# Second expert layer with one 512-column product per hidden slice, and new durations in the planner

## The chip, the cores and the metric

The kernel runs on one core of a Trainium2 chip. The metric is device time in microseconds (us) of one execution; shown is the median of several runs. Engines go by the names of the profile: PE is TensorE (PEld its weight loads), DVE is VectorE, ACT is ScalarE, POOL is GpSimd, SP issues most of the transfers.

## The reference, cut to what matters

Two stages. The first mixes tokens in the frequency domain: x of shape (8, 2496, 256) goes through a real FFT along the sequence, a complex 256 x 256 matrix with bias, a soft threshold and the inverse FFT. The second is a mixture of 8 experts with greedy routing of all 19968 tokens, and that is what the change touches:

```python
cap = N // E                              # 2496 tokens for each expert
order = np.argsort(-logits.flatten())     # best (token, expert) pair first
# a pair is taken if the token is free and the expert has room
for e in range(E):
    mask = assigned == e
    h = np.maximum(x[mask] @ w1[e], 0.0)  # 256 -> 1024
    out[mask] = h @ w2[e]                 # 1024 -> 256
```

## The kernel before, in words

**Stages.** `phase_a` does the spectral part batch by batch with products against DFT matrices, through DRAM scratch tensors T1 and T2, and writes the mixed tokens to YD and their gate logits to LG. `Router` finds, by counting and bisecting on VectorE (`count`, `search`, `bisect`), which tokens each expert gets. `Experts` gathers those tokens, runs both layers and scatters the rows to the output.

**Experts.** There are 16 jobs: for each expert an early one of 512 tokens, from the first half of the batches, and then a late one of 1984 tokens. A job is cut into chunks of up to 512 tokens. `fetch` gathers tiles of 128 tokens (L597, on POOL). `xpose` transposes them (L614), and ScalarE and VectorE split the result into a high and a low part (L617, L618). `ffn1` makes one slice of 128 hidden units with three products of up to 512 columns for each half of the 256 inputs (L629): high weights x high tokens, high x low, low x high. ScalarE writes the rectified high part hh (L633), VectorE the low part hl (L634). `ffn2` makes the output of one tile of 128 tokens: four steps (`qr`) of two hidden slices each, three products of 256 columns per slice, into one PSUM tile `pso` (L646); then ScalarE copies it to SBUF (L650) and POOL scatters it by an indirect transfer (L654). `pso` has two buffers, the output tile `os` has eight.

```python
for a, w_ in ((hh, 0), (hh, 1), (hl, 0)):
    T.matmul(ps.t[0:M], lhsT=a.t[:, 128 * q:128 * q + M], rhs=W2.t[:, w_, ft], start=k == 0, stop=k == 23)
```

W2 holds the high half of the weights as `W2[:, 0]` and the low half as `W2[:, 1]`, eight slices of 256 columns each.

**Order of the work.** The order on every engine is fixed when the program is built. `Plan.run` simulates the engines: each task has an engine, an assumed duration, a position `pos`, and what it reads and writes. At each step it gives the engine that is free first the task that can start first, ties going by `pos`, and for VectorE and POOL within a small hold. The instructions are emitted in that order, and each engine works its queue off in it. So an assumed duration moves no instruction's own time, but can move the order. `K.t` adds a task for TensorE, `v` one for VectorE with 0.068 + n/960 us, `plan.add('A', ...)` one for ScalarE.

**Start.** Batch 0's input comes in 6 chunks of 3 transfers (L1038). Where `(c + j) % 2` is odd they are issued by ScalarE's queue, else by SP's, in the order of the chunks; the DFT matrix for them is issued by ScalarE first (L938). The first DFT (L1062) goes through two PSUM buffers `p15`, which ScalarE and VectorE empty in turn (L1072, L1074). SP stores the results to T1 (L1077) and loads them back transposed as `sh` (L1083); the second DFT (L1096) reads `sh`. L1115 is the product with the complex weights.

**Lists.** For a late job `lists` turns a prefix sum into token numbers: products L479 and L496, sign activations and copies on ScalarE (L501, L502), and some arithmetic on VectorE that ends in the list `li` (L510, L511).

## Time and profile before

| | us |
|---|---|
| median of 3 runs | 1575.0 (1574.66 to 1575.14) |
| the profiled execution | 1583.92 |
| its span, first to last instruction | 1582.1 |
| PE busy in it | 1534.2 |
| DVE busy | 1076.8 |
| ACT busy | 856.0 |
| POOL busy | 669.2 |

The profiled execution is longer than the runs shown by 8.9 us. Products are pipelined, so that the duration of one (about 280 ns for 256 columns) is longer than the distance from its start to that of the next, and a busy PE is not one at its peak. The distance between starts is what a product costs in a stream. Idle time of an engine that is not the bound costs nothing by itself.

### The profile page before, as it was taken

To read this page: it belongs to the slowest core of one execution; us is meant where nothing else is said; L and a number is where in the kernel's file an instruction comes from. 1 tells how busy PE (TensorE), PEld (TensorE's weight loads), DVE (VectorE), ACT (ScalarE), POOL (GpSimd) and SP (SyncE) were. 2 spreads that over 40 slices of the span, in tenths; PEclk is the share of its full clock that TensorE was granted. 3 is DMA by queue.
4 is the path that set the end of the run, shared out by engine and by line. 5 is a ranking of instruction groups with operands and counts; after the bars stand their busy time and mean duration, and the time that the engine had idled before them with its cause. 6 is when DMAs were issued, how large, how long until landed. Compare 5 with 4: busy or idle time off the path is not lost.

```text
span 1582.1 us, 31579 instructions
## 1 busy us (share of the span) xinstructions
PE 1534.2 (97%) x10967; PEld 1362.7 (86%) x10967; DVE 1076.8 (68%) x3451; ACT 856.0 (54%) x1870; POOL 669.2 (42%) x891
## 2 busy tenths in 40 slices
PE   7999999999899989999899999999999999999998
PEld 4999999999787866888788989988998989979997
DVE  3677667677985654789988889887877765453321
ACT  2768888787678776444535234344343443553332
POOL 2236566564636644221334334434334344333332
PEclk8999999999999999999999999999999999999999
DMA  8777777877668666333213122121311212311110
GB/s 256 194 242 248 220 248 215 255 234 229 222 200 257 191 204 182 124 107 114 91 38 101 44 66 71 49 87 55 97 37 51 87 52 83 106 46 42 44 48 28
DMA packets 144201, 208.24 MB, mean 132 GB/s; under 512 B 28751, under 2 KB 108575, under 8 KB 144030
## 3 DMA queue, kind: packets, MB, share of 16 engines
q1 hardware_dynamic: 126776, 161.02, 33.1%
q0 software_dynamic: 16656, 43.77, 8.9%
q8 instruction: 88, 1.44, 0.4%
q10 hardware_dynamic: 598, 1.33, 0.3%
q14 instruction: 83, 0.68, 0.2%
HBM read 121.31 MB, written 84.75 MB: 130 GB/s over the span
## 4 chain that ended last, share of the span: by engine, by line
PE 79%; DVE 7%; DMA 5%; issue 5%; ACT 2%; POOL 1%; SPq 0%; ACTq 0%; POOLq 0%; DVEq 0%
PE ps L646 25%; PE ps L629 16%; PE ps L1115 10%; PE p L629 8%; PE ps L1096 4%; PE ps L1131 3%; PE p L1055 2%; PE p L1162 2%; PE ps L614 2%; PE pt L1185 2%; PE p L1166 1%; PE p L496 1%; PE ps L1203 1%; DVE junk L414 1%; POOL out_dram L654 1%
## 5 line engine op out<-in xcount | busy, mean ns | idle before, releaser
L1115 PE MATMUL ps<-wt,xTh 128*128 128x256 f32 x1280 | 243.4, 288 | 0.2 <-DVE y L1123 0.2
L1115 PEld LDWEIGHTS ps<-wt,xTh 128*128 128x128 f32 x1280 | 198.8, 189 | 8.1 <-issue 3.0
L1115 PE MATMUL ps<-wt,xTl 128*128 128x256 f32 x640 | 179.0, 280 | 0.0
L654 POOL DMA_INDIRECT out_dram<-xTh,li x64 | 65.7, 1026 | 264.6 <-ACT xTh L650 236.4
L414 DVE SCALAR_TENSOR_TENSOR junk<-h_m,st,h_AG 128x156 bf16<-128x156 f32 (+1 forms) x472 | 159.0, 384 | 2.8
L932 POOL TENSOR_TENSOR zl<-y,zh 128x512 fp32r<-128x512 f32 x80 | 106.7, 1334 | 117.3 <-ACT zh L929 110.3
L1192 POOL TENSOR_TENSOR yTl<-yr,yTh 128x468 bf16<-128x468 f32 (+1 forms) x88 | 97.5, 1109 | 93.6 <-ACT yTh L1191 85.1
L1115 PEld LDWEIGHTS ps<-wt,xTl 128*128 128x128 f32 x640 | 120.5, 188 | 0.2 <-DVE xTl L1108 0.2
L654 POOL DMA_INDIRECT out_dram<-xTl,li x64 | 66.0, 1032 | 92.9 <-ACT xTl L650 75.7
L1096 PE MATMUL ps<-FG,sh 128*128 128x128 f32 x640 | 98.0, 282 | 4.5 <-DMA sh<-T 4.5
L646 PE MATMUL ps<-FG,yTh 128*128 128x256 f32 x464 | 97.9, 282 | 0.0
L1096 PEld LDWEIGHTS ps<-FG,sh 128*128 128x128 f32 x640 | 87.4, 194 | 11.9 <-DMA sh<-T 4.7
L650 ACT COPY xTl<-ps 128x256 f32<-128x256 f32 x80 | 29.8, 372 | 124.7 <-PE ps L646 104.6
L646 PE MATMUL ps<-FG,y 128*128 128x256 f32 (+1 forms) x444 | 96.8, 281 | 0.0
L932 POOL TENSOR_TENSOR s2l<-s2c,s2h 120x512 fp32r<-120x512 f32 (+2 forms) x60 | 77.7, 1300 | 35.9 <-DVE s2h L929 27.0
L650 ACT COPY xTh<-ps 128x256 f32<-128x256 f32 x80 | 29.9, 374 | 110.9 <-PE ps L646 93.2
L932 DVE TENSOR_TENSOR xl<-xt,xh 117x512 fp32r<-117x512 f32 (+1 forms) x66 | 66.9, 1015 | 23.8 <-ACT xh L929 23.0
L1106 DVE TENSOR_TENSOR xTl<-ps,xTh 128x512 fp32r<-128x512 f32 x80 | 54.8, 685 | 39.0 <-ACT xTh L1105 38.3
L646 PEld LDWEIGHTS ps<-FG,yTh 128*128 128x128 f32 x464 | 73.3, 185 | 1.4 <-issue 0.2
L646 PE MATMUL ps<-FG,s2c 128*128 128x256 f32 (+1 forms) x336 | 74.1, 281 | 0.0
L646 PEld LDWEIGHTS ps<-FG,y 128*128 128x128 f32 (+1 forms) x444 | 72.2, 185 | 1.9
L646 PE MATMUL ps<-FG,yTl 128*128 128x256 f32 (+1 forms) x312 | 73.8, 280 | 0.0
(708 smaller groups left out, 5053.3 us busy)
## 6 DMA issues: line engine op xcount, KB each, us to landing
xt<-in_moe_w_dram SPq DMA_DIRECT2D x64, 512.0 KB
T<-s4st SPq DMA_DIRECT2D x80, 256.0 KB
sh<-T SPq DMA_DIRECT2D x39, 512.0 KB
s2c<-T SPq DMA_DIRECT2D x80, 240.0 KB
YD<-yst SPq DMA_DIRECT2D x80, 234.0 KB
T<-s1st SPq DMA_DIRECT2D x73, 240.0 KB
xt<-in_x_dram SPq DMA_DIRECT2D x105, 156.0 KB
LG<-lgst SPq DMA_DIRECT2D x80, 21.9 KB
```

The source lines that it names most:

```text
L414: v(cols + 59 + 1400 * K.extra, p, lambda k=k: V.scalar_tensor_tensor(junk[k % 2].t[:, 0:cols], H.m[:, 0:cols], c.t[:, k // ng:k // ng + 1 ...
L614: T.transpose(ps.t[:, 128 * q:128 * q + 128], xg[t // 2].t[:, t % 2, 128 * m:128 * m + 128], H.idn)
L629: T.matmul(ps.t[:, 0:w], lhsT=W1.t[:, a, m, 128 * ft:128 * ft + 128], rhs=x_.t[:, 0:w], start=q + m == 0, stop=q + m == 3)
L646: T.matmul(ps.t[0:M], lhsT=a.t[:, 128 * q:128 * q + M], rhs=W2.t[:, w_, ft], start=k == 0, stop=k == 23)
L650: plan.add('A', .27, pos + 1, lambda: A.copy(o.t[0:M], ps.t[0:M]), [ps], [o])
L654: ins = P.indirect_dma_start(out=self.out, out_offset=bass.IndirectOffsetOnAxis(ap=oi.t[0:M, oo + t:oo + t + 1], axis=0), in_=o.t[0:M], in ...
L932: lambda: eng.tensor_tensor(lb[1](), src(), hb[1](), op=OP.subtract), [srcb, hb[0]], [lb[0]])
L1096: T.matmul(ps.t[:, i, 128 * dt:128 * dt + 128], lhsT=sh.t[:, k, 128 * dt:128 * dt + 128], rhs=Ft.t[:, k], start=True, stop=True)
L1106: plan.add('V', dve(512), pos, lambda th=th, tl=tl, src=src, apart=apart: apart(V.tensor_tensor(cols(tl, 64, 192), src(), cols(th, 64, 192 ...
L1115: T.matmul(ps3.t[:, i], lhsT=a.t[:, i, dt, o:o + 128], rhs=wt[c].t[:, w, dt], start=n == 0, stop=n == 11)
L1131: T.matmul(ps4.t[:, i], lhsT=Gt[p // 8].t[:, g, (2 * p + i) % 16], rhs=v.t[:, i], start=n == 0, stop=n == 2)
L1192: yq.append(plan.add('P', pool(2 * W), pos + 0.376, lambda yh=yh, yl=yl, yr=yr, W=W: P.tensor_tensor(yl.t[:, :, 0:W], yr.t[:, :, 0:W], yh. ...
```

## The change

In `ffn2` a hidden slice now takes two products instead of three. The high part hh is loaded once and multiplied with both halves of the weights in one product of 512 columns, whose result fills a whole PSUM bank: columns 0 to 255 get hh x high weights, columns 256 to 511 hh x low weights. The low part hl times the high weights is accumulated onto the first half as before. ScalarE copies the second half to the output tile, then VectorE adds the first half to it in place. The token `ob` makes the addition wait for the copy.

Assumed durations of the planner are changed in many places, and batch 0's input loads are now all issued by SP.

```diff
         def ffn2(c, q, pos):
...
-            ps, o = K.psum("pso", [128, 256]), K.sb("os", [128, 256])
+            ps, o = K.psum("pso", [128, 2, 256]), K.sb("os", [128, 256])
+            ob = plan.buf(None, None)
             for qr in range(4):
                 def mm(qr=qr):
-                    k = 6 * qr
                     for ft in range(2 * qr, 2 * qr + 2):
-                        hh, hl = hT[c, ft]
-                        for a, w_ in ((hh, 0), (hh, 1), (hl, 0)):
-                            T.matmul(ps.t[0:M], lhsT=a.t[:, 128 * q:128 * q + M], rhs=W2.t[:, w_, ft], start=k == 0, stop=k == 23)
-                            k += 1
-                last = K.t(.652, pos + .5 * qr, mm, [W2] + [x for ft in range(2 * qr, 2 * qr + 2) for x in hT[c, ft]], [ps])
+                        hh, hl = [a.t[:, 128 * q:128 * q + M] for a in hT[c, ft]]
+                        if ft == 7: T.matmul(ps.t[0:M, 0], lhsT=hl, rhs=W2.t[:, 0, ft], start=False, stop=False)
+                        T.matmul(ps.t[0:M], lhsT=hh, rhs=W2.t[:, :, ft], start=ft == 0, stop=ft == 7)
+                        if ft < 7: T.matmul(ps.t[0:M, 0], lhsT=hl, rhs=W2.t[:, 0, ft], start=False, stop=False)
+                last = K.t(.696, pos + .5 * qr, mm, [W2] + [x for ft in range(2 * qr, 2 * qr + 2) for x in hT[c, ft]], [ps])
             self.steps.append(last)
-            plan.add('A', .27, pos + 1, lambda: A.copy(o.t[0:M], ps.t[0:M]), [ps], [o])
+            plan.add('A', .27, pos + 1, lambda: A.copy(o.t[0:M], ps.t[0:M, 1]), [ps], [o, ob])
+            v(256, pos + 1, lambda: V.tensor_tensor(o.t[0:M], ps.t[0:M, 0], o.t[0:M], op=OP.add), [ps, ob], [o])
...
-                turn = not b and (c + j) % 2
-
-                def em(t=t, j=j, m=m, g0=g0, turn=turn):
+                def em(t=t, j=j, m=m, g0=g0):
...
-                    (nc.scalar if turn else nc.sync).dma_start(t.t[39 * j:39 * j + 39, 0:m, :], src)
+                    nc.sync.dma_start(t.t[39 * j:39 * j + 39, 0:m, :], src)
```

The other assumed durations, before and after: the count products .12 to .146; in `lists` the first product .1 to .12, the list products .09 n to .083 + .058 n, the signs .29 to .385 (plus the columns), the copies .06 to .15; the spacer copy on POOL .15 to .28; a chunk's transposes .118 n to .083 + .089 n; an `ffn1` step 3w/2400 + .012 to .018 + 3w/2286; in the early lists .09 nt to .083 + .037 nt; the closing's two small products .05 to .146; in the spectral stage the split after a ScalarE copy + .2, the DFT products 3n/2400 + .02 to .028 + 3n/2286, the complex product 1.42 to 1.47, the rectifying activation + .1, the inverse product 0.715 to 0.745, the transposes 0.42 to 0.4, the gate products .47 + .12 each to .62 + .04 each.

## Rows read from the trace of the kernel before

**Rows 1.** The page: busy us of each engine, share of the span, instructions.
```profile
PE 1534.2 (97%) x10967; PEld 1362.7 (86%) x10967; DVE 1076.8 (68%) x3451; ACT 856.0 (54%) x1870; POOL 669.2 (42%) x891
```

**Rows 2.** Busy us in two stretches: stretch, length, PE, PEld, DVE, ACT, POOL, PEclk, DMA share, GB/s.
```profile
0.00:31.70 31.70, 21.43 (x60) 8.56 (x60) 8.49 (x48) 6.33 (x10) 5.75 (x16) 0.93 0.82 235
...
300.00:400.00 100.00, 98.39 (x799) 90.62 (x798) 73.76 (x124) 80.20 (x159) 57.17 (x46) 1.00 0.75 226
```

**Rows 3.** The page: the chain that ended last, by engine and by line.
```profile
PE 79%; DVE 7%; DMA 5%; issue 5%; ACT 2%; POOL 1%; SPq 0%; ACTq 0%; POOLq 0%; DVEq 0%
PE ps L646 25%; PE ps L629 16%; PE ps L1115 10%; PE p L629 8%; PE ps L1096 4%; PE ps L1131 3%; PE p L1055 2%; PE p L1162 2%; PE ps L614 2%; PE pt L1185 2%; PE p L1166 1%; PE p L496 1%; PE ps L1203 1%; DVE junk L414 1%; POOL out_dram L654 1%
```

**Rows 4.** Copies of finished tiles, L650: count, ns min/median/max, first and last start, forms.
```profile
L650 ACT COPY xTh<-ps x80: 362/373/385, 626.7 to 1572.4; 128x256 f32<-128x256 f32 x80
L650 ACT COPY xTl<-ps x80: 363/373/385, 627.4 to 1575.2; 128x256 f32<-128x256 f32 x72, 64x256 f32<-64x256 f32 x8
```

**Rows 5.** Pieces of the chain that ended last: start us, us, what, how many products.
```profile
635.12 2.73 PE ps L629 x12
...
640.82 2.75 PE ps L629 x12
...
647.11 1.39 PE p L629 x6
...
945.97 9.90 PE ps L646 x84
```

**Rows 6.** Groups of VectorE: shape, count, busy us, mean ns, idle before.
```profile
L1108 DVE TENSOR_TENSOR xTl<-xTh,ps 128x256 fp32r<-128x256 f32 x80 | 32.7, 409 | 0.0
```

**Rows 7.** Busy us from 660 to 960, all engines, columns as in the second group.
```profile
660.00:960.00 300.00, 293.77 (x1977) 259.88 (x1976) 265.93 (x1162) 128.56 (x275) 99.39 (x160) 0.99 0.26 85
```

**Rows 8.** The same stretch for L646 alone: PE, PEld, PEclk, DMA share, GB/s.
```profile
660.00:960.00 300.00, 148.39 (x1152) 142.69 (x1152) 0.99 0.26 85
```

**Rows 9.** All engines from 740 to 760, columns as in the second group.
```profile
740.00:760.00 20.00, 18.17 (x126) 15.48 (x126) 19.89 (x62) 9.31 (x21) 5.08 (x7) 1.00 0.28 84
```

**Rows 10.** Timeline of the end: start, us, engine, line, operation, idle before and releaser.
```profile
1575.16 0.37 ACT L650 COPY xTl<-ps 64x256 f32<-64x256 f32 x1 [2.43 <-PE ps L646]
1575.80 0.91 POOL L654 DMA_INDIRECT out_dram<-xTl,li  x1 [1.73 <-ACT xTl L650]
```

**Rows 11.** Timeline of the start; SPq and ACTq are issues of transfers.
```profile
0.75 0.84 SPq L1038 DMA_DIRECT2D xt<-in_x_dram  x2
...
1.43 0.31 ACTq L1038 DMA_DIRECT2D xt<-in_x_dram  x1
1.63 6.79 SPq L1038 DMA_DIRECT2D sh<-in_x_dram  x7
...
1.78 9.29 ACTq L1038 DMA_DIRECT2D sh<-in_x_dram  x8
...
11.10 1.28 ACT L1072 ACT_TABLE_LOAD   x1 [11.10 <-DMA sh<-in_x_dram]
...
13.03 9.16 PE L1062 MATMUL p<-sh,xh 117*120 117x512 f32 x16 [3.13 <-ACT s4st L1072]
...
26.22 3.09 SPq L1083 DMA_DIRECT2D sh<-T  x6
...
31.73 0.58 PE L1096 MATMUL ps<-FG,sh 128*128 128x128 f32 x1 [4.52 <-DMA sh<-T]
```

**Rows 12.** The page: transfer queues, packets, MB, share of 16 engines' span.
```profile
q1 hardware_dynamic: 126776, 161.02, 33.1%
...
q10 hardware_dynamic: 598, 1.33, 0.3%
```

**Rows 13.** Waits of PE: total us, times, longest.
```profile
PE p L496 <- ACT jl L502: 5.8, 6, 2.6
```

**Rows 14.** Timeline around one list: its last step, and the first transposes after it.
```profile
981.02 0.17 DVE L511 TENSOR_SCALAR li<-li 128x6 int32<-128x6 f32 x1
...
992.53 0.38 PE L614 MATMUL ps<-h_idn,y 128*128 128x128 f32 x2
```

More of the change, by code (lines that the diff above doesn't have):

```diff
@@ L614, in tr @@
                         T.transpose(ps.t[:, 128 * q:128 * q + 128], xg[t // 2].t[:, t % 2, 128 * m:128 * m + 128], H.idn)
-                K.t(.118 * nt, pos + .5 * m, tr, [H.b_idn] + [xg[t] for t in range(2 * c, 2 * c + (nt + 1) // 2)], [ps])
+                K.t(.083 + .089 * nt, pos + .5 * m, tr, [H.b_idn] + [xg[t] for t in range(2 * c, 2 * c + (nt + 1) // 2)], [ps])
                 w = 128 * nt
@@ L630, in ffn1 @@
             for m in range(2):
-                last = K.t(3 * w / 2400 + .012, pos + .5 * m, lambda m=m: mm(m), [W1] + xT[c][m], [ps])
+                last = K.t(.018 + 3 * w / 2286, pos + .5 * m, lambda m=m: mm(m), [W1] + xT[c][m], [ps])
             self.steps.append(last)
```

36 lines of the change are left out of this document (18 added, 18 removed).

## The prediction

> **What bounds the kernel now.** I first read the busy shares [rows 1]: TensorE is busy for 97% of the span, VectorE for 68%. Then the stretches [rows 2]: in the first 31.7 us TensorE works for only 21.43 us, while the DMA share is 0.82; from there on it is nearly always busy (98.39 us of 100 in one stretch of the spectral stage). The chain that ended last [rows 3] agrees: 79% of it is TensorE, and the product of the second expert layer (L646) is with 25% its largest piece. So what counts first is time per product on TensorE, then the 10.3 us that it idles at the start, then whatever makes it wait. TensorE is busy 1534.2 us in all [rows 1], so after the start it is idle for 1582.1 - 31.7 - (1534.2 - 21.4) = 37.6 us, some 7 of them behind the last product.
>
> All sums are against the profiled execution, 1583.9 us (its span of 1582.1 and 1.8 around it). The median of the runs is 1575.0, 8.9 lower; I take the same differences off that. A measurement here can tell about 0.2%, 3.2 us, from no change.
>
> **The new product.** There are 80 + 80 = 160 token tiles [rows 4], each with 8 hidden slices, so 1280 slices. Before, a slice takes three products of 256 columns; after, one of 512 and one of 256. The columns are the same 768; what can be saved is what a product costs beyond its columns. An unbroken run of 84 products of 256 columns takes 9.90 us, 117.9 ns each; runs of 12 products of 512 columns (the first layer, L629) take 2.73 and 2.75 us, 227.5 and 229.2 ns each, and one of 6 into the bank named p takes 1.39, 231.7 each [rows 5]. A slice costs 3 x 117.9 = 353.7 ns before. After, with 229.2, it costs 347.1: 6.6 ns less, **8.4 us over 1280 slices**. The bounds are the other two rows: 227.5 gives 10.6 us, 231.7 gives 5.2. I take the middle row, since the new product writes a bank of the ps kind, as those runs do. All of it lies on TensorE's queue, in stages where TensorE is the bound.
>
> The Trainium skill (TensorE: Matmul & The Clock Gate, section Back-to-back issue gap) gives an isolated product at full clock N / 2.4 + 2.5 ns, hence a fixed part of only 2.5 ns. By that a slice would save 2.5 ns and the kernel 3.2 us; the 117.9 ns here, against 109.2 by the formula, speak for the larger part.
>
> **What VectorE gets.** 160 new additions of 128 x 256 with one operand in PSUM. The nearest row is the 128 x 256 subtraction from PSUM in L1108, 409 ns [rows 6]: 65 us of new work. ScalarE's copy stays, on the other half (373 ns [rows 4]). The addition waits for that copy; queued behind it on VectorE are the counts of the router's search and the low halves of the hidden layer, and for it wait the scatter on POOL (with the next gathers behind it) and TensorE, because the PSUM bank is free only then. There are two such banks and a tile takes 8 x 0.347 = 2.8 us, so a tile's bank is wanted again 2.8 us after its last product, and copy plus addition take 0.8: VectorE may be up to 2 us late before TensorE stops. Late in the kernel that is free. From 660 to 960 us it need not be: there VectorE is busy 265.9 us of 300 [rows 7], and 1152 / 24 = 48 tiles of the second layer run there [rows 8], which adds 48 x 0.409 = 19.7 us. That makes 285.6 of 300. The idle 34 us cover it only where they come at the right time. In the fullest 20 us VectorE was busy 19.89 and TensorE lost 1.83 [rows 9]. Bounds: 0 if all is covered, 19.7 if none is. I take 3 us, a sixth, because two banks let an addition slide by 2 us. At the very end the last tile's addition adds one more step: copy at 1575.16, scatter 1575.80 [rows 10], now with 0.4 between and a hand-over, 0.5 us, fully exposed.
>
> **The loads at the start.** Of batch 0's 18 input loads 9 were issued by ScalarE: 1 and then 8 in 9.29 us, beside 2 and then 7 on SP in 6.79 us [rows 11]. Behind them in ScalarE's queue stood its first table load (11.10 us) and its first PSUM copy, and for that copy TensorE waited 3.13 us, until 13.03 [rows 11]. With all 18 on SP this wait goes. Late next is the data itself, then the 11 stores and 6 loads behind it on SP (the last group begins at 26.22 and ends the stage [rows 11]). So the gain is at most the 3.1 us of the wait as far as these rows show; with the DMA share at 0.82 [rows 2] not all of it can come through. I take 2 us. On the other side, if one queue kept only its own pace of 6.79 / 7 = 0.97 us a load, the 16th would be issued at 1.63 + 16 x 0.97 = 17.2 instead of after ScalarE's 11.07, 6.1 us later. I think little of that: q1 is the queue that stays, q10 moved 1.33 MB in the whole execution [rows 12], and without q10 the stretch from 300 to 400 us still moved 226 GB/s [rows 2].
>
> The Trainium skill (DMA: Bandwidth & Descriptors, section Issuing engines are not separate DMA queues) says that issuing from several engines only saves the sequencers' issue time, as all queues run on the same 16 engines. By that rule the 6.1 us would shrink to issue time alone.
>
> **The new durations in the planner.** They move no work by themselves, but each queue's order is laid out from them, so every wait in the kernel may change. What they mend can be read: the list products L496 waited 5.8 us for ScalarE's copies and signs [rows 13], which the model had too short (0.06 and .29 where it now has .15 and .385). I take 2 us of gain here, bounds of 5.8 gained and 5.8 lost; a new order can as well make such waits.
>
> **Sum:** -8.4 (product) - 2 (start) - 2 (order) + 3 (VectorE) + 0.5 (end) = -8.9 us. 1583.9 becomes 1575.0 in a profiled execution, and the median 1575.0 becomes **1566.1 us**.
>
> **The rivals.**
> *The cost of a product goes by columns.* If the 512 columns cost 2 x 117.9 = 235.8 ns, the product saves nothing and the change doesn't do what it says; the rest of the sum leaves 1574.5. For it speaks that the p row is already at 231.7, against it that long runs of 512 columns stand at 227.5 to 229.2 [rows 5]. Chance 0.10. The skill's formula above is the mild form of it, 1566.1 + 8.4 - 3.2 = 1571.3 by that page.
> *VectorE becomes the bound* (the other side). Place: 660 to 960 us, where the search for the next expert's tokens, the low halves and now the additions share VectorE. It decides once more than about half of the 19.7 us is not covered, since the gains are 12.4. The lists come just in time: one was written at 981.02, and the transposes of its tokens started at 992.53 [rows 14], some gathers later; so a late search turns into a late expert. With all 19.7 exposed: 1566.1 + 16.7 = 1582.8 us. For it: 95% load. Against it: the search is spread by the planner's positions, the planner knows of the additions, and TensorE was idle only 6.2 us in those 300 with VectorE at 89% [rows 7]. Chance 0.16.
> *The order gains more.* If the better durations and the free ScalarE queue take a third of the 30 us of idle time between start and end, 10 instead of 2, and the start gives its full 3.1: 1566.1 - 8 - 1.1 = 1557.0. Chance 0.14.
> *One queue is too slow at the start.* 6.1 us later instead of 2 earlier: 1574.2. Chance 0.05.
> My forecast, 1561 to 1571 by the bounds of its terms, has 0.55.
>
> **How the numbers follow.** Faster by over 0.2% (under 1571.9): the forecast and the better order, with a little of the columns rival: 0.71. Within 0.2%: the columns rival, the slow queue and the edge of VectorE's: 0.14. Slower (over 1578.1): 0.15, nearly all VectorE's. The range goes from 1556, just below the better order, to 1579, which holds the two rivals near 1574 and the mild half of VectorE's; outside are its full price and a better order still.
>
> **What would show it.** Products of L646: starts of a pair 345 to 350 ns apart, 2560 of them instead of 3840; a pair at 354 shows the columns rival. First TensorE work on sh before 30 us (31.73 before), with no wait for ScalarE near 13 us. VectorE busy some 65 us more, near 95% from 660 to 960 us; if TensorE's idle time there grows by over 8 us, or its waits name VectorE or the new addition, the VectorE rival is right. Waits of L496 for ScalarE below 5.8 us. I am wrong if the time is over 1575, or if it is under 1560 with the product's saving below 8 us.

## The result, and the profile after

The kernel after takes **1589.3 us** (median of 6 runs), the kernel before 1575.1 (6 runs): ratio 1.0091, 95% interval 1.0075 to 1.0107. It is slower by 14.3 us, where 1566.1 was forecast. The profiled execution of after took 1589.6 us. The experiments ran on several chips, and on two of them the kernel before takes 1584 to 1586 us in place of 1574 to 1575 (the profile shown ahead of the prediction, 1583.9, fits those two, but its chip is not on record). So times are compared on one chip, and by ratio only between chips of the same kind. Those 10 us do not fall on every kernel alike: e12, which is after but for two assumed durations, takes 1589.8 us on a slow chip, and after 1589.3 on a fast one.

The page of after: span, busy us of each engine, and the chain by engine.

```profile
span 1587.8 us, 29194 instructions
...
PE 1531.5 (96%) x9687; PEld 1293.0 (81%) x9687; DVE 1126.9 (71%) x3611; ACT 855.8 (54%) x1870; POOL 662.3 (42%) x891
...
PE 69%; DVE 12%; DMA 9%; issue 4%; ACT 3%; POOL 2%; SPq 1%; POOLq 0%; DVEq 0%; ACTq 0%
```

TensorE is busy for hardly less than before (1531.5 against 1534.2 [rows 1]) with 1280 products fewer. VectorE has 50 us more (65 were forecast; the additions sum to 67 by their own durations, but neighbours overlap). In the chain TensorE falls from 79 to 69% and VectorE and DMA rise from 7 and 5 to 12 and 9 [rows 3]: the time went into waits. Which ones, the waits of TensorE in after tell (us in total, times, longest):

```profile
PE ps L1095 <- DMA sh<-T: 10.1, 6, 4.2
PE ps L614 <- DVE s2c L618: 3.2, 1, 3.2
...
PE ps L629 <- DVE yr L634: 2.4, 1, 2.4
```

The line numbers of the spectral stage are one lower than before, so L1095 is the first product on sh, L1096 before. It waited once before, 4.5 us, at the start [rows 11]; now six times, once at the start and five times between batches, 6.0 us in all for the five.

**The start** did what was wanted. Timeline of after:

```profile
1.42 1.28 ACT L1071 ACT_TABLE_LOAD   x1 [1.42 <-PEq L1454]
2.05 8.56 SPq L1037 DMA_DIRECT2D sh<-in_x_dram  x15
...
24.52 2.73 SPq L1082 DMA_DIRECT2D sh<-T  x6
...
27.46 0.80 PE L1095 MATMUL ps<-FG,sh 128*128 128x128 f32 x2 [4.18 <-DMA sh<-T]
```

ScalarE loads its table at 1.42 in place of 11.10, TensorE's wait for its copy is gone, and sh is used at 27.46 in place of 31.73 [rows 11]. SP issues 15 loads in 8.56 us, 0.57 us each, not the 0.97 of the slow-queue rival.

**The product** saved little. Timeline of one tile's chain in after, TensorE alone:

```profile
902.82 0.40 PE L646 MATMUL ps<-FG,yTh 128*128 128x512 f32 x1
903.05 0.28 PE L647 MATMUL ps<-FG,s4st 128*128 128x256 f32 x1
903.18 0.40 PE L646 MATMUL ps<-FG,yTl 128*128 128x512 f32 x1
...
904.59 0.39 PE L646 MATMUL ps<-FG,s2c 128*128 128x512 f32 x1
...
904.94 0.28 PE L645 MATMUL ps<-FG,xh 128*128 128x256 f32 x1
```

From 902.82 to 904.94 are six pairs, 353 ns each (starts 0.23 and 0.12 us apart), where 347 was forecast and three products of 256 columns took 353.7. This tile is at the slow end: over the 831 pairs of the trace that follow each other without a break at full clock the median is 351 ns (the middle eight tenths from 344 to 357) and the mean 350.4; three products of 256 columns have 353 by both in e0. (In either kernel some 100 starts come about 85 ns late; the means leave them out.) So a slice saves 2 to 2.7 ns, and the kernel 2.6 to 3.5 us. By the prediction's own test (345 to 350 for its forecast, 354 for the rival) that lies between the two, and nearer in worth to the columns rival.

**The stages.** Below, the spectral stage runs from the first product on sh to the first product of the first expert layer, the expert stage from there to the end of the last product of the second. After has 557.7 and 994.7 us. The kernel before, run again as e0 (time 1575.1), has 547.3 and 986.2. The start gains 5.2, the two stages lose 10.4 and 8.5. Busy us of after and then of e0 in three stretches (columns as in [rows 2]):

```profile
660.00:960.00 300.00, 295.46 (x1611) 240.33 (x1610) 281.14 (x1215) 131.39 (x281) 95.69 (x159) 1.00 0.26 84
960.00:1300.00 340.00, 330.15 (x1813) 273.04 (x1812) 275.70 (x1188) 140.66 (x359) 130.20 (x225) 0.99 0.20 62
...
585.20:1579.90 994.70, 972.48 (x5306) 798.77 (x5304) 727.43 (x2808) 422.33 (x971) 363.83 (x610) 1.00 0.25 76
```

```profile
660.00:960.00 300.00, 294.98 (x1990) 261.17 (x1989) 268.38 (x1167) 129.59 (x278) 98.68 (x160) 1.00 0.26 84
960.00:1300.00 340.00, 338.55 (x2321) 306.02 (x2321) 266.06 (x1161) 144.76 (x367) 134.07 (x226) 1.00 0.20 63
...
580.00:1566.30 986.30, 972.06 (x6587) 867.58 (x6585) 678.69 (x2649) 422.67 (x971) 369.19 (x610) 1.00 0.24 77
```

In the stretch that I had feared, 660 to 960, VectorE is at 94% and TensorE loses nothing. The loss is at 960 to 1300: TensorE is idle there for 9.9 us against 1.5, with VectorE at only 81%. So VectorE's load alone can't be it.

### The profile page after: what moved, and what is told of

Read it like the earlier page. It is cut to its first block, busy times and chain, and to the rows that moved or that the text cites. A ratio compares the mean times of both kernels' runs of the same rounds, so it can differ in the third digit from the quotient of the medians.

```text
span 1587.8 us, 29194 instructions
## 1 busy us (share of the span) xinstructions
PE 1531.5 (96%) x9687; PEld 1293.0 (81%) x9687; DVE 1126.9 (71%) x3611; ACT 855.8 (54%) x1870; POOL 662.3 (42%) x891
## 4 chain that ended last, share of the span: by engine, by line
PE 69%; DVE 12%; DMA 9%; issue 4%; ACT 3%; POOL 2%; SPq 1%; POOLq 0%; DVEq 0%; ACTq 0%
PE ps L629 15%; PE ps L646 14%; PE ps L1114 9%; PE p L629 7%; PE ps L647 6%; PE ps L1095 3%; PE ps L1130 2%; PE p L1054 2%; DMA xt<-in_moe_w_dram 2%; PE ps L614 2%; DMA sh<-T 2%; PE p L1161 2%; PE pt L1184 1%; DVE junk L414 1%; DMA lo<-LG 1%
## 5 line engine op out<-in xcount | busy, mean ns | idle before, releaser
L1114 PE MATMUL ps<-wt,xTh 128*128 128x256 f32 x1280 | 244.7, 289 | 0.1
L1114 PEld LDWEIGHTS ps<-wt,xTh 128*128 128x128 f32 x1280 | 199.6, 190 | 8.3 <-issue 4.2
L1114 PE MATMUL ps<-wt,xTl 128*128 128x256 f32 x640 | 179.5, 280 | 0.5 <-DVE xTl L1107 0.5
L1114 PEld LDWEIGHTS ps<-wt,xTl 128*128 128x128 f32 x640 | 121.1, 189 | 0.7 <-DVE xTl L1107 0.7
L1095 PE MATMUL ps<-FG,sh 128*128 128x128 f32 x640 | 97.8, 283 | 10.3 <-DMA sh<-T 10.1
L1095 PEld LDWEIGHTS ps<-FG,sh 128*128 128x128 f32 x640 | 87.1, 194 | 20.1 <-DMA sh<-T 11.2
L650 ACT COPY xTl<-ps 128x256 f32<-128x256 f32 x80 | 29.8, 372 | 116.3 <-PE ps L646 101.5
L650 ACT COPY xTh<-ps 128x256 f32<-128x256 f32 x80 | 29.9, 374 | 113.2 <-PE ps L646 89.0
L933 DVE TENSOR_TENSOR xl<-xt,xh 117x512 fp32r<-117x512 f32 (+1 forms) x66 | 61.0, 925 | 31.9 <-ACT xh L930 31.3
L1122 DVE SCALAR_TENSOR_TENSOR y<-ps,y 128x512 f32<-128x512 f32 x80 | 55.0, 687 | 28.0 <-ACT y L1121 26.8
L651 DVE TENSOR_TENSOR xTl<-ps,xTl 128x256 f32<-128x256 f32 x80 | 33.6, 420 | 56.5 <-ACT xTl L650 56.2
L1189 DVE TENSOR_TENSOR yr<-pt,yTh 128x468 f32<-128x468 f32 (+1 forms) x77 | 47.9, 623 | 31.7 <-ACT yTh L1188 31.5
L629 PE MATMUL ps<-yTh,sh 128*128 128x512 f32 (+1 forms) x193 | 70.2, 393 | 0.0
L1120 DVE TENSOR_TENSOR ps<-ps,bt 128x512 f32<-128x512 f32 x80 | 55.4, 692 | 15.9 <-PE ps L1114 15.7
L1190 ACT CAST yTh<-yr 128x468 bf16<-128x468 f32 (+1 forms) x88 | 50.6, 576 | 24.7 <-DVE yr L1189 24.4
```

Source lines behind the costliest of these rows:

```text
L629: T.matmul(ps.t[:, 0:w], lhsT=W1.t[:, a, m, 128 * ft:128 * ft + 128], rhs=x_.t[:, 0:w], start=q + m == 0, stop=q + m == 3)
L650: plan.add('A', .27, pos + 1, lambda: A.copy(o.t[0:M], ps.t[0:M, 1]), [ps], [o, ob])
L933: lambda: eng.tensor_tensor(lb[1](), src(), hb[1](), op=OP.subtract), [srcb, hb[0]], [lb[0]])
L1095: T.matmul(ps.t[:, i, 128 * dt:128 * dt + 128], lhsT=sh.t[:, k, 128 * dt:128 * dt + 128], rhs=Ft.t[:, k], start=True, stop=True)
L1114: T.matmul(ps3.t[:, i], lhsT=a.t[:, i, dt, o:o + 128], rhs=wt[c].t[:, w, dt], start=n == 0, stop=n == 11)
L1120: plan.add('V', dve(512), pos + 1.282, lambda ps3=ps3: V.tensor_tensor(ps3.t, ps3.t, bt[:, None, :].to_broadcast([128, 2, 256]), op=OP.add ...
```

## The experiments

The change has four parts that can be made alone: the product with its addition; the queue of the loads; the new durations of the spectral stage; those of counts, lists, gather, transposes and the first expert product (the expert durations). All runs (times in us, ratio to before on the same chip; the last column is what ScalarE waited in all for loads of weights):

| run | what it has | median | before | ratio, 95% interval | spectral | expert | weights |
|---|---|---|---|---|---|---|---|
| e0 | before | 1574.9 | 1574.6 | 0.9998, 0.9984 to 1.0011 | 547.3 | 986.2 | 6.1 |
| e1 | product | 1576.3 | 1574.6 | 1.0012, 1.0001 to 1.0024 | 546.3 | 987.6 | 4.1 |
| e2 | all durations | 1580.0 | 1574.6 | 1.0029, 1.0011 to 1.0047 | 557.1 | 980.0 | 8.2 |
| e3 | queue | 1571.0 | 1574.6 | 0.9976, 0.9961 to 0.9991 | 547.4 | 988.2 | 5.9 |
| e4 | product, all durations | 1595.4 | 1584.2 | 1.0078, 1.0058 to 1.0097 | 552.8 | 994.4 | 20.6 |
| e5 | spectral durations | 1587.3 | 1584.2 | 1.0026, 1.0014 to 1.0038 | 553.8 | 988.8 | 8.1 |
| e6 | expert durations | 1576.5 | 1584.2 | 0.9951, 0.9937 to 0.9966 | 545.4 | 987.7 | 7.5 |
| e7 | product, expert durations | 1580.4 | 1584.2 | 0.9974, 0.9961 to 0.9986 | 543.7 | 993.4 | 18.4 |
| after | all four | 1589.3 | 1575.1 | 1.0091, 1.0075 to 1.0107 | 557.7 | 994.7 | 21.5 |
| e8 | after, addition on 8 columns | 1581.8 | 1574.8 | 1.0048, 1.0030 to 1.0066 | 560.7 | 988.8 | 20.0 |
| e9 | after, L1114 at 1.42 | 1588.6 | 1574.8 | 1.0087, 1.0067 to 1.0107 | 554.8 | 997.2 | 20.1 |
| e10 | queue, expert durations | 1565.6 | 1574.8 | 0.9935, 0.9917 to 0.9952 | 551.9 | 983.0 | 11.1 |
| e11 | after, product in halves | 1581.8 | 1574.8 | 1.0041, 1.0027 to 1.0054 | 559.3 | 989.9 | 14.4 |
| e12 | after, copy and addition planned as measured | 1589.8 | 1585.6 | 1.0027, 1.0014 to 1.0039 | 558.7 | 995.8 | 18.7 |
| e13 | product, queue, expert durations | 1579.8 | 1585.6 | 0.9971, 0.9959 to 0.9984 | 546.2 | 995.9 | 17.5 |
| e14 | e13, product in halves | 1582.6 | 1585.6 | 0.9988, 0.9977 to 0.9998 | 547.1 | 993.4 | 12.8 |
| e15 | e13, copy and addition planned as measured | 1578.2 | 1585.6 | 0.9951, 0.9936 to 0.9966 | 548.0 | 994.2 | 15.9 |
| e16 | e13, weights' low parts on GpSimd | 1655.6 | 1573.8 | 1.0522, 1.0494 to 1.0550 | 548.2 | 1067.9 | 7.4 |
| e17 | e10, weights' low parts on GpSimd | 1649.1 | 1573.8 | 1.0466, 1.0440 to 1.0492 | 552.7 | 1062.6 | 6.1 |

The stages are of one trace each, and a few us of them are chance: e8 and e11 have after's order of work and, in the spectral stage, its very instructions, and show 560.7 and 559.3 there for 557.7.

### The parts alone: e0 to e3

e0 is the kernel before. e1 is the product with its addition, with the step's old duration:

```diff
-                            T.matmul(ps.t[0:M], lhsT=a.t[:, 128 * q:128 * q + M], rhs=W2.t[:, w_, ft], start=k == 0, stop=k == 23)
...
+                        T.matmul(ps.t[0:M], lhsT=hh, rhs=W2.t[:, :, ft], start=ft == 0, stop=ft == 7)
...
+            v(256, pos + 1, lambda: V.tensor_tensor(o.t[0:M], ps.t[0:M, 0], o.t[0:M], op=OP.add), [ps, ob], [o])
```

e2 is every new duration, of which two lines stand here, with the step of the old product at 0.707; e3 is the loads of x on SP alone:

```diff
-            plan.add('T', 1.42, pos + 0.7 + .3 * i, mm3, [th, tl] + wt, [ps3])
+            plan.add('T', 1.47, pos + 0.7 + .3 * i, mm3, [th, tl] + wt, [ps3])
...
-                last = K.t(.652, pos + .5 * qr, mm, [W2] + [x for ft in range(2 * qr, 2 * qr + 2) for x in hT[c, ft]], [ps])
+                last = K.t(.707, pos + .5 * qr, mm, [W2] + [x for ft in range(2 * qr, 2 * qr + 2) for x in hT[c, ft]], [ps])
...
```

```diff
-                    (nc.scalar if turn else nc.sync).dma_start(t.t[39 * j:39 * j + 39, 0:m, :], src)
+                    nc.sync.dma_start(t.t[39 * j:39 * j + 39, 0:m, :], src)
```

> The kernel before, unchanged, for a second profile of it. The profiled execution shown with it (1583.9 us) lies 8.9 us over the median of its runs (1575.0). If that was that one execution's own, the new profile lies within 3 us of the runs' median, and its spectral stage is some microseconds shorter. If profiling itself costs 9 us, the new one is near 1584 again. The median of the runs should be 1575 within 2 us.

> The new product and its addition alone, with the assumed duration of its step left at .652, every other duration and the loads as before. Theory A (the new order of the spectral and list work costs the time): the product and the addition are worth a few microseconds at most, 1571 to 1578 us. Theory B (the product with its addition on VectorE costs the time): 1583 to 1590 us, with TensorE's waits naming VectorE from 600 us on.

> All new assumed durations, the old product (its step set to .707, what six products of 256 columns take), the old loads. Theory A: most of the loss is here, 1583 to 1591 us, with waits at the batch boundaries of the spectral stage. Theory B: 1571 to 1577 us.

> All input loads of batch 0 on SP, nothing else changed. The second DFT begins 4 us earlier (27.5 instead of 31.7 us after the start of the span). If that is carried to the end, 1571 us; if the next batch's loads and stores give it back, 1574 to 1576. A third theory, that this reordering is the loss, says 1583 or more.

**Measured:** e0's own profiled execution took 1575.1 us, so profiling itself doesn't cost 9. The product alone gains nothing (1.0012), the durations cost 5.4 us (between e2's two theories), the queue gains 3.6. The three sum to +3.5 us; all together cost 14.3. TensorE's busy time in the expert stage doesn't tell the product's part. It is 972.06 in e0 (above) and 970.02 in e1, but 977.48 in the profile shown ahead of the prediction, of the same kernel as e0; e1, then that profile:

```profile
579.20:1566.90 987.70, 970.02 (x5307) 799.59 (x5305) 727.40 (x2808) 422.58 (x971) 361.83 (x610) 1.00 0.24 77
...
579.30:1575.10 995.80, 977.48 (x6587) 870.21 (x6585) 678.26 (x2649) 423.15 (x971) 369.73 (x610) 0.99 0.24 76
```

The distances between starts are steadier: a pair has a median of 351 ns in e1 as in after, so the 2.6 to 3.5 us hold here too. The Trainium skill (TensorE: Matmul & The Clock Gate, Back-to-back issue gap) gives an isolated product a fixed part of 2.5 ns, from which 3.2 us can be estimated. The trace agrees that the fixed part is small; the products themselves (starts 0.12 and 0.23 us apart) take longer than its 109 and 216 ns.

### What interacts: e4 to e7

e4 is the kernel after with the loads on two queues again. e5 has only the durations of the spectral stage, e6 only the expert durations, e7 the latter with the product. e5 and e6 have besides, as e2 has, the old product's step at 0.707 in place of 0.652, so the expert order of e5 isn't that of before either.

```diff
-            plan.add('T', 0.715, pos + 1.15, mm4, [zh, zl, BG_[part(GQ, 2 * p)]], [ps4], uses=[Gt[p // 8]])
+            plan.add('T', 0.745, pos + 1.15, mm4, [zh, zl, BG_[part(GQ, 2 * p)]], [ps4], uses=[Gt[p // 8]])
...
```

```diff
-                last = K.t(3 * w / 2400 + .012, pos + .5 * m, lambda m=m: mm(m), [W1] + xT[c][m], [ps])
+                last = K.t(.018 + 3 * w / 2286, pos + .5 * m, lambda m=m: mm(m), [W1] + xT[c][m], [ps])
...
```

> The product with its addition and all new durations; the loads of x on two queues as before. Theory (the loss lies in the product's addition meeting the order that the new durations make): the queue change has no part in it and only keeps its own gain of 3.6 us away, so about 1589 + 3.6 = 1593 us, PE idle in the expert stage 18 to 24 us. Rival (the three edits only add up, and the rest comes from a plan that moves with the queue): 1574.9 + 1.7 + 5.4 = 1582 us, and PE idle in the expert stage about 12 us.

> The new durations of the spectral stage alone (transforms, channel product, gate, transposes and its two additions to ScalarE and split), all else as before. Theory (these move the loads of sh to the end of a batch behind their product): the first DFT2 to the first product of the experts takes 557 us in place of 547, waits for sh about 10 to 13 us in six places, in all about 1575 + 10 = 1585 us. Rival (the durations of the lists of tokens, which share engines with the spectral stage, cause it): 547 us and about 1575 us.

> The new durations of counts, lists, Sign, gather, transposes and first expert product alone, and the second product's step at 0.707 with the product of before. Theory: the expert stage gains what it gained with all durations (986 to 980 us), the spectral stage stays at 547 us: about 1569 us. Rival (the gain in the expert stage came from the spectral stage ending later, so that lists were ready earlier against it): no gain, about 1575 us.

> The same expert durations with the new product and its addition, spectral durations and queues as before. Theory (the addition and the new expert order together make VectorE late with low parts and counts): PE idle in the expert stage 18 to 24 us against 9 in the kernel without the product, expert stage 990 to 995 us, in all about 1569 + 12 = 1581 us. Rival (the loss needs the spectral durations too): expert stage 980 to 984 us, about 1570 us.

**Measured:** the loss needs no queue change (e4). The spectral durations lengthen their stage (e5: 553.8 us, waits for sh 12.6 us in five places, of which 5.8 at the start and 6.8 between batches). As a whole e5 loses only 3.1 us, where 10 were expected; its expert stage is 988.8, and since the chips differ, what before has there on this one is not known. The expert durations gain 7.7 us (e6). With the product added they gain only 3.9 (e7), and the expert stage goes from 987.7 to 993.4. With the spectral durations added too it is 15.0 us more (e7 to e4, same chip), of which the spectral stage has 9.1. So there are **two losses**: the spectral durations (in company; alone they cost 3.1), and the product in the new expert order.

**Why the spectral durations cost time.** Between two batches, the last first transform (L1055) is copied, stored (L1077) and loaded again (L1083) before the first product on sh (L1096). The same stretch of e0, then of e5:

```profile
278.60 0.39 PE L1055 MATMUL p<-xh,d 78*80 78x512 f32 x1
...
279.64 0.32 SPq L1077 DMA_DIRECT2D T<-s1st  x1
283.25 2.40 SPq L1083 DMA_DIRECT2D sh<-T  x5
288.96 0.61 PE L1096 MATMUL ps<-FG,sh 128*128 128x128 f32 x4
```

```profile
280.10 0.39 PE L1055 MATMUL p<-xh,d 78*80 78x512 f32 x1
...
282.30 0.32 SPq L1077 DMA_DIRECT2D T<-s1st  x1
285.07 2.41 SPq L1083 DMA_DIRECT2D sh<-T  x5
290.85 0.71 PE L1096 MATMUL ps<-FG,sh 128*128 128x128 f32 x4 [1.62 <-DMA sh<-T]
```

From the transform to the product on sh are 10.4 us in e0 and 10.8 in e5. In e0 TensorE has work for all of it and doesn't wait, but only just: at the first five of its seven batch ends the load is through 0.9 us or less before its use. 48 products of L1115 and 12 of L1131 stand between, beside transforms and transposes. In e5 there are 36 and 12: one channel product of 12 x 0.117 us, 1.4 us, has moved behind, since the plan now thinks each longer (e9, below, puts it back), and the store begins 2.2 us after the transform in place of 1.0. The plan was made more exact on TensorE, and not on the transfer that it had to cover. These waits, 6.0 us in after, are the larger part of the 10.4 that its stage is longer, not all of it: TensorE's other waits there grow from 10.2 (e0) to 12.0 us, and the rest is not traced.

### Load or order, and one duration back: e8 to e11

e8 makes the addition on 8 columns (its text says what it leaves out), e9 puts the channel product's duration back, e11 cuts the 512-column product in two. e10 has only the two parts that gained.

```diff
-            v(256, pos + 1, lambda: V.tensor_tensor(o.t[0:M], ps.t[0:M, 0], o.t[0:M], op=OP.add), [ps, ob], [o])
+            v(256, pos + 1, lambda: V.tensor_tensor(o.t[0:M, 0:8], ps.t[0:M, 0, 0:8], o.t[0:M, 0:8], op=OP.add), [ps, ob], [o])
```

```diff
-            plan.add('T', 1.47, pos + 0.7 + .3 * i, mm3, [th, tl] + wt, [ps3])
+            plan.add('T', 1.42, pos + 0.7 + .3 * i, mm3, [th, tl] + wt, [ps3])
```

```diff
-                        T.matmul(ps.t[0:M], lhsT=hh, rhs=W2.t[:, :, ft], start=ft == 0, stop=ft == 7)
+                        for a in [slice(0, 2)] if ft in (0, 7) else [0, 1]: T.matmul(ps.t[0:M, a], lhsT=hh, rhs=W2.t[:, a, ft], start=ft == 0, stop=ft == 7)
```

e10 is the diff of e3 and that of e6 together.

> The kernel after, with the addition made on 8 columns in place of 256 (it leaves out the first half's share of the other 248); plan and order of every instruction stay as they are. Theory (order: the addition's step pushes low parts, lists and counts to places in VectorE's queue where they come late): PE idle in the expert stage stays at 18 to 22 us and the time at about 1588 us. Rival (load: the 0.42 us that each of 160 additions takes make VectorE late): idle falls to about 10 us, expert stage from 994.7 to about 983 us, in all about 1577 us.

> The kernel after, with the channel product's duration back at 1.42. At a batch's end the channel product that the new duration moved behind the first DFT2 then stands ahead of it again. Theory (that one product, 2.75 us, was the cover of the store and load of sh): waits for sh fall from 10 us in six places to about 3 to 5 us, the spectral stage from 558 to about 550 us, in all about 1582 us. Rival (the other spectral durations lengthen the stage, and the waits for sh are only where that shows): 556 to 558 us, about 1589 us.

> The loads of x on SP's queue, and the new durations of counts, lists, gather, transposes and first expert product; product and spectral durations as before (the second product's step at 0.707). Theory (the parts that gain are independent of those that lose): start 4 to 5 us earlier, spectral stage 546 to 548 us, expert stage 986 to 988 us, about 1571 us, ratio to before 0.990 to 0.998. Rival (without the product the order of the expert stage depends on when the spectral stage ends, so a start 5 us earlier undoes the gain): expert stage 993 us or more, about 1577 us.

> The kernel after, with the high part's 512-column product cut into two products of 256 columns in six of every eight slices (960 of 1280); plan, order of the steps and addition stay. Theory (512 columns take 232 ns and two of 256 take 2 x 117.8 = 235.6): about 960 x 3.5 ns = 3.4 us longer at most, about 1592 us. Rival (the figure of the prediction, 6.6 ns a slice): 6.3 us longer, about 1595.5 us.

**Measured.** *e8* falls between the two: 6.8 us less than after by ratio, the expert stage 988.8, against 994.7 with the whole addition and 983.0 in e10, which has none (its profiled execution, 1586.3, is 4.5 above its median, so the stages shown are long). What the addition really costs VectorE is in its group (busy us, mean ns, then the idle time of VectorE just ahead of it); after, then e8:

```profile
L651 DVE TENSOR_TENSOR xTh<-ps,xTh 128x256 f32<-128x256 f32 x80 | 33.7, 422 | 38.4 <-ACT xTh L650 35.3 <-issue 2.7
L651 DVE TENSOR_TENSOR xTl<-ps,xTl 128x256 f32<-128x256 f32 x80 | 33.6, 420 | 56.5 <-ACT xTl L650 56.2
```

```profile
L651 DVE TENSOR_TENSOR xTh<-ps,xTh 128x8 f32<-128x8 f32 x80 | 13.1, 164 | 42.9 <-ACT xTh L650 42.8
```

The 160 additions take 67 us, and VectorE stands another 95 us ahead of them, until TensorE has finished the tile and ScalarE has copied it (L650), with everything queued behind; cutting the addition does not cut that wait. It is not 95 us more of idle time: in the expert stage VectorE stands 267 us in after and 308 in e0. What counts is which steps it holds up. As e11, below, gains as much without a change on VectorE, e8 by itself doesn't show that the addition's time is the cause.

*e9* restores the order at the batch's end (48 and 12 again), and the waits for sh fall from 10.1 to 6.0 us, but the spectral stage keeps 7.5 of its 10.4 us, and the expert stage is 2.5 longer: the time stays (1.0087). One duration was a part of the cause, not the cause; that theory fell.

*e10* beats both kernels: 0.9935, 9.3 us under before. It has no product, and its list products wait 0.3 us for ScalarE (5.8 before [rows 13], 3.0 in e0). Its ratio was expected, its spectral stage was not: 551.9, where e3 and e6 have 547.4 and 545.4. So the parts that gain are not independent either.

*e11* is a surprise: the product in halves should cost some 3 us and is 7.9 us faster than after by ratio. Both run the same steps in the same order, on ScalarE, VectorE and GpSimd without a difference. In the expert stage the traces part mainly in one place: from 1051 to 1076 us VectorE's steps in after fall back by 3.6 us against e11, and by another 1.2 near 1150. The first place in after, then in e11:

```profile
1039.57 10.97 SPq L569 DMA_DIRECT2D xt<-in_moe_w_dram  x4
...
1048.81 1.22 DVE L577 TENSOR_TENSOR sh<-xt,sh 128x1024 fp32r<-128x1024 f32 x1
...
1056.63 1.05 ACT L576 CAST FG<-xt 128x1024 fp32r<-128x1024 f32 x1 [3.10 <-DMA xt<-in_moe_w_dram]
1057.71 1.23 DVE L577 TENSOR_TENSOR FG<-xt,FG 128x1024 fp32r<-128x1024 f32 x1 [2.86 <-ACT FG L576]
1058.86 0.68 DVE L634 SCALAR_TENSOR_TENSOR yr<-ps,yTh 128x512 fp32r<-128x512 f32 x1
...
1059.59 0.50 PE L629 MATMUL ps<-zl,sh 128*128 128x512 f32 x1 [2.38 <-DVE yr L634]
```

```profile
1056.24 1.05 ACT L576 CAST FG<-xt 128x1024 fp32r<-128x1024 f32 x1 [1.22 <-DMA xt<-in_moe_w_dram]
...
1059.21 0.50 PE L629 MATMUL ps<-zl,sh 128*128 128x512 f32 x1 [0.35 <-DVE yr L634]
```

This is a **chain of queues**: ScalarE stands 3.1 us for the weights of the next expert (L576); VectorE, whose next step is their low part (L577), stands 2.9; the low half of the hidden layer (L634) comes after that, and TensorE, which needs its bank, stands 2.4. In e11 the last weights come 0.4 us earlier, TensorE gets there later, and its wait is 0.35; in e8 it is 1.70. (The profiled execution of e11 was its slowest, 1586.4 against 1581.8, so it shows only a part of the gain.) Why the weights are late can be read from the first two lines: the four pieces share two buffers, and the issue of the fourth ends at 1050.54, half a microsecond after VectorE's low part of the second (1048.81 + 1.22). So VectorE, late with one low part, is late with the next again. The last column of the table is 4 to 11 us where the product or the expert durations are missing and 16 to 22 where both are there (e11 and e14 have 14.4 and 12.8, the two kernels at the end less), but it doesn't rank the expert stages: e8 has 20.0 with 988.8. That VectorE's standing at the additions starts this chain is argued, not shown by an experiment. Nor is the chain the product's price in every plan: e7 and e13 wait as long for weights (18.4 and 17.5), and TensorE has no wait over 1 us there between 1000 and 1180 us.

The other large wait of after is VectorE's order alone:

```profile
1292.35 0.59 ACT L617 CAST s2c<-ps 128x512 fp32r<-128x512 f32 x1 [1.38 <-PE ps L614]
1292.43 0.18 DVE L525 TENSOR_SCALAR li<-li 128x16 f32<-128x16 f32 x1
...
1295.42 0.17 DVE L535 SCALAR_TENSOR_TENSOR li<-or,or 128x16 int32<-128x16 f32 x1
1295.52 0.68 DVE L618 TENSOR_TENSOR s2c<-ps,s2c 128x512 fp32r<-128x512 f32 x1
...
1296.26 0.52 PE L614 MATMUL ps<-h_idn,yTl 128*128 128x128 f32 x2 [3.25 <-DVE s2c L618]
```

ScalarE's high part is written by 1292.94, but the low part (L618) stands behind the small steps of a list, L525 to L535, some 3 us, and the transposes wait 3.25 us for their bank. This place is common to the kernels with product and expert durations. TensorE's waits for the low part L618 in the expert stage sum to 6.1 to 7.3 us in e4, e7, after, e9 and e11 to e14 (4.2 in e15; in e8 2.3, and 3.3 more that the profile puts down to the addition behind it), to 4.4 in e1, and to 2.2 to 3.8 in the six with the old product (e16 and e17 left out). On one chip, the tile copies of e7 are 1.0 us behind those of e6 at 1271 us, 3.5 at 1307 and 5.8 at 1423. So the product's price in the new expert order begins here, in the order of VectorE's queue. Which step of the plan makes that order was not isolated.

### What was open after these: e12 to e15

e12 is after with the copy and the addition planned as measured; e13 is after with the old spectral durations; e14 is e13 with e11's diff; e15 is e13 with e12's.

```diff
-            plan.add('A', .27, pos + 1, lambda: A.copy(o.t[0:M], ps.t[0:M, 1]), [ps], [o, ob])
-            v(256, pos + 1, lambda: V.tensor_tensor(o.t[0:M], ps.t[0:M, 0], o.t[0:M], op=OP.add), [ps, ob], [o])
+            plan.add('A', .375, pos + 1, lambda: A.copy(o.t[0:M], ps.t[0:M, 1]), [ps], [o, ob])
+            plan.add('V', .42, pos + 1, lambda: V.tensor_tensor(o.t[0:M], ps.t[0:M, 0], o.t[0:M], op=OP.add), [ps, ob], [o])
```

> The kernel after, with the plan told 0.375 us for ScalarE's copy ahead of the addition and 0.42 us for the addition. Theory (the plan's short durations put the addition where VectorE stands for the copy, and weights, low parts and lists behind it come late): VectorE's idle time ahead of the additions falls from 95 to under 60 us, PE idle in the expert stage from 21.8 to about 14 us, about 1580 us. Rival (VectorE's position does not hang on these 0.19 us): idle 85 us or more ahead of the additions, and 1586 to 1592 us.

> The full change less the durations of the spectral stage: loads of x on SP, product with addition, durations of counts, lists, gather, transposes and first expert product. Theory (the spectral durations cost about 10 us, the product with the new expert order about 6 to 8 us): spectral stage 546 to 548 us, expert stage 992 to 995 us, ratio to before 1.001 to 1.004, about 1578 us. Rival (what the spectral stage loses comes back later whatever its order): 1.006 or more, over 1584 us.

> The kernel of e13 with six of every eight 512-column products cut in two of 256; plan and order the same. Theory (512 columns are 3.5 ns cheaper a slice, and the gain of e11 was one late weight that it met or missed): 2 to 4 us longer than e13. Rival (the 512-column product costs time in itself, by what it holds back on other engines): 5 to 8 us shorter than e13, as e11 against the kernel after.

> The kernel of e13 with 0.375 us for the copy and 0.42 us for the addition in the plan. Theory: expert stage 984 to 988 us and about 1570 us, level with the kernel that leaves the product out (ratio 0.994 to 0.998). Rival: as e13.

**Measured.** *e12 against e15*, which differ in the spectral durations alone: 11.6 us, of which the spectral stage has 10.7. With e7 to e4 that is the second pair, and the loss is settled. *e13:* the expert stage is as long as in after (995.9), so that loss needs only product and expert durations; since before may itself have 995.8 on such a chip, e6 to e7 is the better evidence. Its ratio, 0.9971, is under both theories. *e14:* in this plan the halves cost 2.8 us, so the 512 columns are no burden in themselves. That e11's gain belongs to the weights that one plan met or missed fits this and the place where e11 parts from after; it was not tried by itself. *e12 and e15:* VectorE still stands 98 and 96 us ahead of the additions; the 0.19 us of plan are worth 1.6 us (e13 to e15). That theory fell: VectorE stands mostly for TensorE's last product of the tile, behind which the copy comes, and no duration of the copy changes that. The order did move: the wait at L614 near 1290 us falls from 3.25 (after) to 1.26 in e12, and from 4.12 (e13) to under 1.3 in e15, but in both three others of 2.0 to 2.3 us come up between 750 and 800.

### VectorE relieved: e16 and e17

The 64 low parts of the weights, 1.22 us each, go from VectorE to GpSimd, in e13 and in e10.

```diff
-                v(1024, p + 1, lambda part=part: K.V.tensor_tensor(part(2), part(0), part(1), op=OP.subtract), [r, h], [W])
+                plan.add('P', 2.3, p + 1, lambda part=part: K.P.tensor_tensor(part(2), part(0), part(1), op=OP.subtract), [r, h], [W])
```

> The kernel of e13 (product, queue, expert durations) with the 64 low parts of the weights (1.22 us each, 78 us together) taken from VectorE and given to GpSimd at about 2.5 us each. Theory (VectorE's time and place in its queue make the expert stage longer): ScalarE's waits for weights fall from 17.5 to under 10 us, expert stage from 995.9 to 984 to 989 us, time 7 to 11 us under e13's share of the kernel before, ratio 0.990 to 0.993. Rival (the loads of weights are late by themselves, or GpSimd's longer low parts free their buffers later still): expert stage 994 us or more, ratio 0.996 or more.

> The kernel of e10 (queue and expert durations, product of before) with the same 64 low parts on GpSimd. Theory (without the addition VectorE has no part in the waits that are left): within 3 us of e10, ratio 0.991 to 0.996. Rival (VectorE's load costs time there too): 5 us or more shorter, ratio 0.990 or less.

**Measured:** both are about 5% slower. For e17 that is outside either theory; e16's rival set no upper bound, but its mechanism (buffers free later still) is not it, as ScalarE's waits for weights fall (17.5 to 7.4 us). VectorE loses elsewhere. Timeline of e16:

```profile
998.55 3.36 DVE L414 SCALAR_TENSOR_TENSOR junk<-h_m,st,wt 128x156 bf16<-128x156 f32 x1
999.30 2.43 POOL L577 TENSOR_TENSOR FG<-xt,FG 128x1024 fp32r<-128x1024 f32 x1
...
1001.85 0.07 DVE L414 DVE_READ_ACCUMULATOR junk<-h_m,st,wt 128x1 f32 x1
```

A count that takes 0.38 us lasts 3.36, until GpSimd's subtraction is through; so do, with 1.98 to 3.36 us, 13 of the 16 counts that overlap one. TensorE waits 22.0 us in all for counts. The experiment says nothing of the addition, as relief and new cost came together; only the pair is left: with the product 6.5 us longer than without, in this plan too.

## Why the prediction was wrong

Three steps failed: the product's saving was mis-sized, the new durations' cost in the spectral stage was put at nothing, and VectorE's price was looked for in the wrong place.

**The product, -8.4: mis-sized.** The step that failed is the price of a product beyond its columns. The 229.2 ns of L629 were right for 512 columns in a run of their own. In front of a 256-column product 512 columns take 232 ns: that is the median in after, and also in the trace of before, at 84 places where a product of L646 follows one of L629. The 231.7 that I took for the lower bound [rows 5] was the right size, and a 256-column product between them takes 118.4 (mean), so a pair is 350 to 351 ns, not 347. TensorE's products save 2.6 to 3.5 us, outside my bounds of 5.2 to 10.6. That 117.9 ns lie over the formula's 109.2 did not speak for a larger fixed part, since 232 lie over its 215.8 by nearly twice as much: the excess goes with the columns. What I set down as the rival *cost by columns*, with a chance of 0.10, was nearly true, and its mild form was the better price: the 3.2 us estimated from the formula of the Trainium skill (TensorE: Matmul & The Clock Gate, Back-to-back issue gap).

**The start, -2: right, and more.** sh is used 4.3 us earlier, beyond my 3.1; alone it is worth 3.6 us (e3). In company it is not kept: e13 has it and stands with e7, which has not, at 0.9971 and 0.9974. The slow-queue rival was wrong: 15 loads were issued in 8.56 us. The Trainium skill (DMA: Bandwidth & Descriptors, Issuing engines are not separate DMA queues) says that issuing from several engines saves only the time of issuing, and the trace agrees: one queue issued at 0.57 us a load.

**The order, -2 with bounds of 5.8: two terms hidden in one.** I costed the new durations by the one wait that I could see them mend. That part was right: the list products' waits fell to 0.7 us, and the expert durations gain 7.7 us (e6), or 6.5 (e3 to e10, ratios 0.9976 to 0.9935). The spectral durations, which I gave no row of their own, cost 11.6 (e15 to e12) to 15.0 us (e7 to e4) beside the product, more than the 5.8 that I allowed for the whole term. The row to read was the end of a batch: 10.4 us from the transform to sh, covered by TensorE's work with mostly 0.9 us or less to spare, so that a new order could easily uncover it.

**VectorE, +3: the place was wrong.** From 660 to 960 us it went as forecast (281.1 of 300 busy, 285.6 worked out) without cost. The price came later, at 960 to 1300 in after: with the product's 2.6 to 3.5 us set against it, the kernel is still 3.9 us longer (e6 to e7) or 6.5 (e17 to e16), in a stretch where VectorE has time to spare. I counted how full VectorE is and how late an addition may be. I left out that the addition stands in VectorE's queue for the tile and ScalarE's copy, 95 us in all, and that the order of that queue changes with it. What came late were the low parts of the gathered tokens (L618), behind a list's small steps, in the plans with product and expert durations, least in e15, and in after the weights' low parts, hence buffers, hence the next loads. Neither was on my list of who is queued there. That the addition's place in the queue, and not another move of the new plan, is the cause is argued. **The end, +0.5:** from the last copy to its scatter 1.09 us in place of 0.64 [rows 10], as forecast.

**The sum** by pairs that differ in one part: queue -3.6 (e3) to -0.5 (e7 to e13), expert durations -7.7 to -6.5, product with addition in the new order +3.9 to +6.5, spectral durations beside it +11.6 to +15.0. That is +4 to +14.5 us, and 14.3 lies at its upper edge. The parts alone don't give it (e5 costs only 3.1): they hold each other's waits, and which late weight meets TensorE changes with half a microsecond (e11). The rival on the other side, VectorE, had the right sign, an engine that the waits name, and the wrong place; the larger loss, loads of sh that the new order uncovers, was in none of the rivals.

## What to carry to other kernels

Making one engine's durations exact in a planner can uncover a transfer that the old, too short ones had covered by luck: put measured times for round trips through memory beside them, or look at the places where a load lands with no slack first. Work added to an engine that is not full still costs where it waits, and for whom its queue is in order: read the idle time ahead of the new step, not only its duration. Price a merged product from rows that alternate as the new code will; here 512 plus 256 columns cost only 2 to 3 ns less than three times 256 (351 against 353), and the best kernel (e10, 0.9935) does without the merged product.

## What the hardware showed

**The clock can fall after a short wait.** Stretches of after behind the 2.4 us wait at 1059.59 (columns as before; PEclk is the third from the right):

```profile
1058.00:1060.00 2.00, 0.41 (x2) 0.36 (x3) 2.00 (x3) 1.15 (x3) 0.17 (x1) 1.00 0.27 66
1060.00:1062.00 2.00, 2.00 (x10) 1.40 (x9) 1.94 (x9) 0.57 (x1) 0.09 (x1) 0.74 0.00 0
1062.00:1064.00 2.00, 2.00 (x8) 1.62 (x7) 1.07 (x6) 0.20 (x2) 0.00 (x0) 0.50 0.00 0
1064.00:1066.00 2.00, 2.00 (x9) 1.59 (x8) 1.17 (x2) 1.01 (x2) 0.00 (x0) 0.91 0.02 4
```

After the wait the granted clock goes to 0.50, the lower of the two levels (1.2 GHz), while TensorE is busy again for all of each stretch. Summing 2 x (1 - PEclk) over the three stretches, an estimate, that takes 1.7 us more, so the wait of 2.4 us costs about 4. e11 fits it: its wait there is 2.0 us shorter, its clock stays at 1.00, and it gains 3.6. Behind the 3.25 us wait at 1296 the clock falls too, to 0.62 and 0.53 in the first two stretches of 2 us. It does not fall behind every such wait: in e8, behind 1.70 us at 1058.47, it stays at 1.00. A wait in the list of waits need not be the whole of its price.

**VectorE stands still while GpSimd reads.** The count of e16 above has two operands in SBUF, and GpSimd's subtraction reads there too. The Trainium skill (SBUF — State Buffer, SBUF: two separate sides) says that such a pair takes turns for a whole instruction on a port that both share, whichever starts first having it. The trace agrees on the turns: 13 counts end 0.2 us after a subtraction, 3.36 us long in this case against 0.38. On who is first it agrees in ten of the 13; in three, this one among them, the profile gives the count the earlier start (998.55 against 999.30), and yet it ends last.

**A chip can hide or make 10 us.** The kernel before took 1574 to 1575 us on three chips and 1584 to 1586 on two, and its expert stage has 986.2 in one trace and 995.8 in another. Over the whole span their clocks are alike (0.992 and 0.991), but not in that stage: TensorE is idle there for 14.2 and 18.3 us, and the granted clock is 0.998 and 0.993, which is, as an estimate, 1.7 and 6.8 us. The two together are 9.2 of the 9.5 us. Why the waits differ was not tried.
